# Left rows of Wo as partial sums per column tile, B rows and output in 128-token tiles, and one filler pass inside Wo, in a segment-recurrent attention kernel

## The chip, the cores and the metric

One core of one Trainium2 chip (trn2). The metric is the device time of one execution in microseconds (us). "Before" and "after" are the kernel without and with the change. Times are medians of several executions. Engines are named as in the profile: PE is TensorE's matmuls, PEld its weight loads, DVE is VectorE, ACT is ScalarE. To evict is to copy a finished product out of its accumulation bank. PV is the product of the attention weights with V; a segment has two, of 16 heads each.

## The reference, cut to what matters

Two attention branches over the same 2048 tokens of width 512 are mixed by a gate. Branch A is recurrent: 64 segments of 32 tokens, each with 8 memory tokens in front, 32 heads of 128. The first 8 output rows of a segment are the memory of the next.

```python
def _A_ref(x, mem0, Wq, Wk, Wv, Wo, seg_len):          # seg_len 32, M 8
    mem = mem0
    for s in range(n_seg):                             # 64, one after the other
        h = concat([mem, x[:, 32*s:32*s+32]], axis=1)  # 40 tokens
        q, k, v = h @ Wq, h @ Wk, h @ Wv               # 32 heads of 128
        p = softmax(where(mask, q k^T * scale, -1e9))
        o = einsum('bhte,hed->btd', p v, Wo)
        mem = o[:, :M]; outs.append(o[:, M:])
# b = _B_ref(...): 4 blocks of 512 tokens, ends in  o @ wo
g = sigmoid((x * gate_w).sum(-1))
return g * a + (1 - g) * b
```

## The kernel before

All of B but its last product is computed first, up to about 355 us. Then the segments run. A segment works on 32 tokens, the 8 memory rows and the first 24 of its own; the last 8 tokens of four segments, 32 rows, are done together as "left rows", in filler passes that stand in the next segments. Four segments make a group (r = 0 to 3 is the place in it). The filler units of a group are spread over 24 slots, six a segment.

A matmul on a token tile of 32 uses 32 columns of TensorE's array (128*32 in the profile's shapes; one on 128 tokens has 128*128), so the kernel works in four column tiles (j) side by side: in the trace before, a set of four matmuls of 512 columns on the four tiles started every 216 ns, and so did single ones of 128*128. For Wo each tile computes another 128 of the 512 output columns:

```python
def wo(b):                      # main Wo; b = 0, 1: heads 0-15, 16-31
    for half in range(2):
        for h in range(16*b + 8*half, 16*b + 8*half + 8):
            for j in range(4):
                pe.matmul(pb[bk][SEG*j:SEG*(j+1), 0:128], OT_sb[:, h, 0:SEG],
                          Wo_sb[:, h, 128*j:128*(j+1)], start=(h == 0), stop=(h == H-1))

def ol_units(g):                # left rows, four filler units of 8 heads
    ...
        for h in range(8*part, 8*part + 8):
            for j in range(4):
                pe.matmul(pb[bk][SEG*j:SEG*(j+1), 0:128], OTL[par][:, h, :],
                          Wo_sb[:, h, 128*j:128*(j+1)], ...)
        # after part 3: 16 matmuls for the left B rows, t1L (ACT), finL (DVE), four stores

# end of a segment
    scores(1); take_fill(2); sums(1)
    bks0 = pv(0)
    ot_ev(0, bks0, 1, "dve"); norm(1); ot_ev(0, bks0, 0, "act")
    brow(...)                   # 16 matmuls, B rows of these 32 tokens
    take_fill(2)
    # ACT: t1 = (1 - g) * B rows
    bks1 = pv(1)
    ot_ev(1, bks1, 0, "dve"); ot_ev(1, bks1, 1, "act")
    wo(0); wo(1)
    # DVE: aW = evicted Wo
    take_fill(1)
    # PE: transpose aW; DVE: its 8 memory columns into hT of the next segment
    take_fill(1)
    # DVE: fin = g * aW + t1; four stores every fourth segment
```

`take_fill(n)` issues the units of the next n slots. A matmul is two instructions, weight load and matmul (33,806 and 33,774 records in the profile before).

The softmax here doesn't subtract the row's maximum and nothing guards it: scores larger than these inputs give would overflow.

## Time and profile before

| | before |
|---|---|
| time, median (range) | 1375.42 us (1368.93 to 1380.39, 4 runs) |
| start of the first segment | 355 us |
| one group of four segments (trace, groups 2 to 15) | 63.6 us |
| TensorE instructions per group | about 3650 |
| instruction packets of 16 KB | 264 |

Lines of the profile's page: the span, busy time by engine with its share and the number of instructions, the DMA queues, and the chain that ended last.

```profile
span 1371.9 us, 72224 instructions
...
PE 1110.0 (81%) x33774; PEld 664.6 (48%) x33806; DVE 591.8 (43%) x1541; ACT 622.3 (45%) x1440; POOL 187.0 (14%) x416
...
q1 hardware_dynamic: 19496, 23.09, 4.9%
q8 instruction: 264, 4.33, 1.3%
...
PE 67%; DVE 11%; ACT 10%; issue 10%; DMA 2%; SPq 0%; POOL 0%; DVEq 0%; ACTq 0%
```

TensorE is the engine to look at. A tenth of the chain is "issue": time in which the engine waited for nothing that the profile knows. 264 packets on q8 for the 67,580 matmuls and weight loads are 256 instructions each.

The view of waits names who waited for whom: total us, number of times, longest.

```profile
PE ps L1088 <- issue: 69.5, 51, 2.1
...
DVE finL_sb L952 <- ACT t1L L949: 24.5, 16, 3.3
...
PE ps L873 <- DVE hT L1146: 15.8, 33, 0.8
...
PE ps L938 <- issue: 12.5, 10, 1.8
PE ps L1052 <- DVE Pn_sb L1040: 10.2, 34, 0.7
PE ps L873 <- issue: 7.3, 9, 1.5
```

L1088 is main Wo, L938 left Wo, L1052 the PV product, L873 the projections. The pauses before Wo come to 69.5 us in 51 pieces.

Matmuls of one segment (r = 0), in order of time: start, length, line, shapes, number; in brackets the idle time before.

```profile
865.15 0.41 PE L968 MATMUL ps<-woB_sb,oT 128*32 128x128 bf16 x16
...
865.94 0.89 PE L938 MATMUL ps<-Wo_sb,OTL 128*32 128x128 bf16 x49 [0.17 <-issue]
866.76 0.27 PE L1052 MATMUL ps<-Pn_sb,V_sb 32*128 32x40 bf16 x16
...
867.05 0.85 PE L1088 MATMUL ps<-Wo_sb,OT_sb 128*32 128x128 bf16 x47
869.27 1.35 PE L1088 MATMUL ps<-Wo_sb,OT_sb 128*32 128x128 bf16 x81 [1.37 <-issue]
...
872.74 0.23 PE L968 MATMUL ps<-woB_sb,oTL 128*32 128x128 bf16 x1 [1.50 <-issue]
```

The pauses cut through runs of identical matmuls whose inputs have long been there, so no data dependency explains them. Set beside the packet times on q8, the longer ones end 1.1 to 1.8 us after an instruction packet has landed: of the 85 weight-load gaps over 0.9 us in the recurrent part 69 do, and the other 16 end with a result of DVE or ACT. Counted in the built program, nearly all stand at the same place modulo 256 instructions: 68 of the 69 at remainder 194 or 195. A pause is therefore TensorE waiting for the next block of its own program. Packets start no closer than about 3.2 us apart and take 1.05 us in the mean, while a Wo of 256 instructions takes 1.8 us unstalled, a matmul every 14 ns. At each of the 68 pauses TensorE had used up all blocks landed, and in no trace did the packet of a block start while TensorE was more than 1.2 blocks short of it (at most 1.11 here).

From this I made one measure, used below as **stall**: at each block end of the recurrent part, the gap between weight loads, less 0.06 us, if it exceeds 0.15 us and ends 1.1 to 1.8 us after a landing. **Rest** is the segment's time less its stall. Both are means over the groups from the second on, by r, and are worked out from the trace; the profile prints neither.

| us | r=0 | r=1 | r=2 | r=3 | group |
|---|---|---|---|---|---|
| stall, before | 3.36 | 1.40 | 1.49 | 1.35 | 7.58 |
| rest, before | 14.30 | 13.94 | 13.56 | 13.84 | 55.63 |

### The profile page before, as it was taken

To read this page: it belongs to the slowest core of one execution; us is meant where nothing else is said; L and a number is where in the kernel's file an instruction comes from. 1 tells how busy PE (TensorE), PEld (TensorE's weight loads), DVE (VectorE), ACT (ScalarE), POOL (GpSimd) and SP (SyncE) were. 2 spreads that over 40 slices of the span, in tenths; PEclk is the share of its full clock that TensorE was granted. 3 is DMA by queue.
4 is the path that set the end of the run, shared out by engine and by line. 5 is a ranking of instruction groups with operands and counts; after the bars stand their busy time and mean duration, and the time that the engine had idled before them with its cause. 6 is when DMAs were issued, how large, how long until landed. Compare 5 with 4: busy or idle time off the path is not lost.

```text
span 1371.9 us, 72224 instructions
## 1 busy us (share of the span) xinstructions
PE 1110.0 (81%) x33774; PEld 664.6 (48%) x33806; DVE 591.8 (43%) x1541; ACT 622.3 (45%) x1440; POOL 187.0 (14%) x416
## 2 busy tenths in 40 slices
PE   4767667676788889888898988898888889798886
PEld 3444445344345555544555554454554455454544
DVE  3556667564343334433343433343433334343433
ACT  3857656474343434433344434343433444343433
POOL 7323222132001000010000000000010000000000
PEclk8988788576899999998999999999999999999999
DMA  9400000001100000000000000000000000000000
GB/s 358 135 2 3 2 2 2 2 2 52 75 4 8 5 6 7 5 7 4 7 5 8 3 9 4 7 7 4 7 5 7 4 8 4 7 4 8 3 7 8
DMA packets 19794, 27.70 MB, mean 20 GB/s; under 512 B 9760, under 2 KB 17960, under 8 KB 17960
## 3 DMA queue, kind: packets, MB, share of 16 engines
q1 hardware_dynamic: 19496, 23.09, 4.9%
q8 instruction: 264, 4.33, 1.3%
q14 instruction: 34, 0.28, 0.1%
HBM read 20.99 MB, written 2.10 MB: 17 GB/s over the span
## 4 chain that ended last, share of the span: by engine, by line
PE 67%; DVE 11%; ACT 10%; issue 10%; DMA 2%; SPq 0%; POOL 0%; DVEq 0%; ACTq 0%
PE ps L873 32%; PE ps L1088 10%; ACT PT_g L662 6%; PE ps L882 6%; PE ps L572 2%; PE ps L653 2%; PE ps L1052 2%; PE ps L938 2%; PE ps L1028 1%; PE ps L1008 1%; DVE OT_sb L865 1%; PE ps L968 1%; PE ps L1061 1%; DVE QTg L576 1%; DMA Wv_sb<-in_A_Wv_dram 1%
## 5 line engine op out<-in xcount | busy, mean ns | idle before, releaser
L662 ACT ACTIVATE PT_g<-ps 128x512 bf16<-128x512 f32 (+1 forms) x384 | 170.3, 529 | 58.1 <-PE ps L653 55.7
L1088 PE MATMUL ps<-Wo_sb,OT_sb 128*32 128x128 bf16 x8192 | 138.4, 220 | 69.6 <-issue 69.5
L1088 PEld LDWEIGHTS ps<-Wo_sb,OT_sb 128*32 128x32 bf16 x8192 | 117.9, 97 | 78.5 <-issue 76.7
L1133 POOL COPY OTL<-OT_sb 128x256 bf16<-128x256 bf16 x64 | 25.8, 403 | 920.1 <-DVE OT_sb L865 920.1
L873 PE MATMUL ps<-Wk_sb,hT 128*32 128x512 bf16 x2048 | 136.3, 406 | 17.7 <-DVE hT L1146 15.8
L873 PE MATMUL ps<-Wq_sb,hT 128*32 128x512 bf16 x2048 | 136.1, 382 | 0.0
L865 DVE CAST V_sb<-ps 128x512 bf16<-128x512 f32 x128 | 88.6, 692 | 110.0 <-PE ps L873 110.0
L873 PE MATMUL ps<-Wv_sb,hT 128*32 128x512 bf16 x2048 | 134.8, 381 | 0.0
L863 ACT ACTIVATE QN_sb<-ps 128x512 bf16<-128x512 f32 x128 | 76.5, 597 | 124.1 <-PE ps L873 124.1
L668 POOL TENSOR_SCALAR_AFFINE_SELECT PT_g<-PT_g 128x512 bf16<-128x512 bf16 x128 | 82.8, 647 | 211.8 <-ACT PT_g L662 209.6
L865 DVE CAST KN_sb<-ps 128x512 bf16<-128x512 f32 x64 | 44.3, 692 | 132.1 <-PE ps L873 132.1
L863 ACT ACTIVATE QT_sb<-ps 128x512 bf16<-128x512 bf16 x128 | 76.4, 597 | 45.4 <-PE ps L882 45.4
L873 PEld LDWEIGHTS ps<-Wk_sb,hT 128*32 128x32 bf16 x2048 | 55.2, 101 | 80.8 <-DVE hT L1146 26.8
L865 DVE COPY KT_sb<-ps 128x512 bf16<-128x512 bf16 x128 | 54.4, 425 | 88.4 <-PE ps L882 88.4
L865 DVE CAST aW_sb<-ps 128x128 bf16<-128x128 f32 x64 | 18.7, 292 | 171.1 <-PE ps L1088 171.1
L865 DVE CAST OT_sb<-ps 128x320 bf16<-128x320 f32 x128 | 63.0, 492 | 52.5 <-PE ps L1061 51.2
L653 PE MATMUL ps<-QTg,KTg 16*128 16x128 bf16 x1280 | 43.0, 244 | 52.1 <-ACT PT_g L662 48.6
L863 ACT ACTIVATE KN_sb<-ps 128x512 bf16<-128x512 f32 x64 | 38.2, 597 | 94.7 <-PE ps L873 94.7
L863 ACT ACTIVATE OT_sb<-ps 128x320 bf16<-128x320 f32 x128 | 55.0, 430 | 50.5 <-PE ps L1061 49.9
L873 PEld LDWEIGHTS ps<-Wq_sb,hT 128*32 128x32 bf16 x2048 | 50.8, 97 | 49.7 <-issue 3.4
L873 PEld LDWEIGHTS ps<-Wv_sb,hT 128*32 128x32 bf16 x2048 | 49.5, 95 | 30.4
L1031 ACT ACTIVATE R_sb<-ps 128x160 f32<-128x160 f32 x128 | 38.9, 304 | 54.4 <-PE ps L1029 54.3
(136 smaller groups left out, 1846.0 us busy)
## 6 DMA issues: line engine op xcount, KB each, us to landing
Wk_sb<-in_A_Wk_dram SPq DMA_DIRECT2D x4, 1024.0 KB, 11.6
Wq_sb<-in_A_Wq_dram SPq DMA_DIRECT2D x4, 1024.0 KB, 20.6
Wo_sb<-in_A_Wo_dram SPq DMA_DIRECT2D x4, 1024.0 KB, 19.7
Wv_sb<-in_A_Wv_dram SPq DMA_DIRECT2D x4, 1024.0 KB, 9.4
x_sb<-in_A_x_dram SPq DMA_DIRECT2D x4, 512.0 KB, 5.5
out_dram<-fin_sb SPq DMA_DIRECT2D x64, 24.0 KB
out_dram<-finL_sb SPq DMA_DIRECT2D x64, 8.0 KB
wqN_sb<-in_B_wq_dram SPq DMA_DIRECT2D x1, 512.0 KB, 7.3
```

The source lines that it names most:

```text
L572: ins = pe.matmul(pb[7][:, 0:LB], wqB_sb[:, c, g * 128:(g + 1) * 128], xT[:, c, T0p:T0p + LB], start=(c == 0), stop=(c == C - 1))
L653: ins = pe.matmul(pb[j][:, 128 * slot:128 * (slot + 1)], KTg[32 * j:32 * j + DH, 128 * kc:128 * kc + 128], QTg[32 * j:32 * j + DH, 128 * q ...
L662: P.op("act", (lambda j=j: (lambda a: a.activation(ptb[:, j, 128 * n0:128 * (n0 + len(wv))], pb[j][:, 0:128 * len(wv)], ACT.Exp, scale=SCA ...
L668: P.op("gp", (lambda n=n: (lambda gq: gq.affine_select(ptb[:, :, 128 * n:128 * (n + 1)], ptb[:, :, 128 * n:128 * (n + 1)], [[0, 4], [1, 128]],
L863: P.op("act", lambda a: a.activation(dst, src, ACT.Copy), reads=[rbank[k] for k in bks], writes=dres, name=name)
L865: P.op("dve", lambda d: d.tensor_copy(dst, src), reads=[rbank[k] for k in bks], writes=dres, name=name)
L873: ins = pe.matmul(pb[bk][SEG * j:SEG * (j + 1), :], lhs(c), w_sb[:, c, n0:n0 + 512], start=(c == 0), stop=(c == C - 1))
L882: ins = pe.transpose(pb16[bk][:, i * 128:(i + 1) * 128], nat[:, b, i * 128:(i + 1) * 128], ident[:, :])
L938: ins = pe.matmul(pb[bk][SEG * j:SEG * (j + 1), 0:128], OTL[par][:, h, :], Wo_sb[:, h, 128 * j:128 * (j + 1)], start=(h == 0), stop=(h == ...
L1031: P.op("act", lambda a: a.activation(R_sb[:, b, :], pb[bk][:, 224:384], ACT.Ln), reads=[rbank[bk]], writes=[Rs("R%d" % b)], name="ln%d_%d" ...
L1052: ins = pe.matmul(pb[bks[j]][:, L * i:L * (i + 1)], V_sb[SEG * j:SEG * (j + 1), b, i * E:(i + 1) * E], Pn_sb[SEG * j:SEG * (j + 1), b, L * ...
L1088: ins = pe.matmul(pb[bk][SEG * j:SEG * (j + 1), 0:128], OT_sb[:, h, 0:SEG], Wo_sb[:, h, 128 * j:128 * (j + 1)], start=(h == 0), stop=(h == ...
```

## The change

The intent: fewer and wider TensorE instructions for the same products, cheaper output, and something other than Wo matmuls in the middle of Wo. Left Wo: each column tile sums 8 of the 32 heads over all 512 columns, 32 matmuls of 512 columns instead of 128 of 128. The four partial sums (rows 32j to 32j+31) are evicted as a bf16 value and its rounding remainder, and a 0/1 matrix `selL` sums the four tiles and transposes at once. B rows: one unit of four matmuls per group on the 128 tokens. The output is collected transposed in `aT_st`, transposed back once per group, gated, and stored with one DMA. One of the two fillers between the PVs moves between `wo(0)` and `wo(1)`. The per-place gates, and the five fp32 matmuls that made them at the start, go. Its core, with cuts marked:

```diff
-                    for h in range(8 * part, 8 * part + 8):
+                    for n in (2 * part, 2 * part + 1):
                         for j in range(4):
-                            ins = pe.matmul(pb[bk][SEG * j:SEG * (j + 1), 0:128], OTL[par][:, h, :],
-                                            Wo_sb[:, h, 128 * j:128 * (j + 1)], start=(h == 0), stop=(h == H - 1))
+                            h = 16 * (n // 4) + 4 * j + n % 4
+                            ins = pe.matmul(pb[bk][SEG * j:SEG * (j + 1), :], OTL[par][:, h, :], Wo_sb[:, h, :],
+                                            start=(n == 0), stop=(n == 7))
...
                 if part == 3:
-                    ... (left B rows, t1L, finL, four stores)
+                    evac("act", LN_sb[:, 0, :], pb[bk], [bk], [rl[0]], "olhi%d" % g)
+                    P.op("dve", lambda d: d.tensor_tensor(LN_sb[:, 1, :], pb[bk], LN_sb[:, 0, :], ALU.subtract), ...)
...
+        def ut():   # 8 matmuls: LN_sb[:, k, 128c:128c+128] with selL -> ACT copies the left columns into aT_st
+        def ub():   # 4 matmuls of 512 columns: B rows; ACT: t1 = (1 - g) * B rows, 128x512
+        def uf():   # 4 transposes of aT_st; DVE: fin = g * aT + t1, 128x512; one store
...
         ot_ev(0, bks0, 0, "act")
-        bb = B.take()
-        brow(bb, lambda f: oT[:, f, SEG * s:SEG * (s + 1)], ...)
-        take_fill(2)
-        P.op("act", ... t1 ...)
+        take_fill(1)
         bks1 = pv(1)
...
         wo(0)
+        take_fill(1)
         wo(1)
...
+        P.op("dve", lambda d: d.tensor_copy(aT_st[par][:, :, SEG * r:SEG * (r + 1) - M], asrc[:, :, M:SEG]), ...)
         take_fill(1)
-        fb = fin_sb
-        P.op("dve", ... fin ...)
-        if r == 3 or s == nseg - 1:
-            ... (four stores)
```

## The prediction

> What bounds it. The change touches the recurrent part, from about 355 us to the end: 64 segments, 15.8 us each. TensorE is the bottleneck: from 500 to 1360 us it was busy 748 of 860 us (windows view), DVE 335, ACT 357. A segment is about 13.8 us of TensorE work and dependency gaps, and up to 2 us of "issue": in the waits view TensorE idled 70 us before the Wo matmuls, 12 before the left-row Wo, 17 before others, 98 us in all, with nothing to wait for. The DMA view names the cause: queue q8, kind instruction, moved 264 packets of 16 KB for 67,600 TensorE instructions, 256 each. A long pause ends about 1.3 us after such a packet, nearly always at the same place of the 256. Wo is 128 matmuls and 128 weight loads in 1.8 us: it eats a block faster than the next arrives. [...]

> What changes, per group of four segments.
> Instructions: left Wo 128 to 32 pairs, B rows 80 to 4, plus 8 for the selecting transpose and 4 for the output transpose: 160 pairs fewer, about 3650 to 3333 instructions, 14.3 to 13.0 blocks. The filler inside Wo (none in one segment of four) lets a block arrive meanwhile.
> Charging each block what a fetch of about 3.5 us exceeds the time of its 256 instructions, I get about 8 us of stall per group before and 3.5 after: gain 4.5 us.
> TensorE work stays nearly equal: left Wo 32 x 57 ns is still 1.8 us, B rows 4 x 216 ns replace 5 x 0.23 us; about 0.5 us of selection and 0.2 us of transposes are new.
> Dependencies get worse. Between first and second PV stands a DVE chain of 1.44 us whatever fills it. Before, the B rows and one or two fillers hid there; now one, and what left (three fillers a group in Wo, 0.5 us each) stands on the path: +1.5 us. In a group's first segment the high/low split (ACT 0.6 us, DVE 0.7 us) precedes the copy of the new memory and the selection: +0.8 us. In the second, the 128x512 t1 (0.6 us) and fin (0.7 us) delay the evictions between the PVs: +1 us. Loss about 3.4 us.
> Net -1.1 us per group, -18 us over 16. At the start five gate selection matmuls (2.3 us) and a copy go: -2.6 us. Tail: zero.

> Predicted 1357 us (-1.6%), 8 in 10 within 1332 to 1380. Faster by over 2%: 0.36; within 2%: 0.60; slower: 0.04.

> Would show it right: instruction packets near 245; issue time before Wo down by more than half; left Wo pauses nearly gone; longer waits of the second PV on DVE and of the next K on hT; about 15.4 us per segment.

> Would make it wrong: if the fetch stall nearly vanishes, the gain is 4%. If it only moves to PV or projection instructions, or the DVE and ACT queues delay the PVs more than I add up, there is no gain. Stalls depend on where blocks end; 3333 is nearly 13 blocks, so these places hardly drift, and a bad one repeats.

The sum: -4.5 us of stall and +3.4 us of loss make -1.1 us per group, -18 us over 16 groups, with -2.6 us at the start. The 3.5 us of a fetch is an estimate; in the recurrent part of the trace before, packets start 3.2 us apart at the least, and one in ten within 3.5 us.

## The result, and the profile after

After: 1338.44 us (1335.08 to 1341.21, 4 runs); before 1375.42 us. The ratio is 0.9733, 95% interval 0.9681 to 0.9785.

The page after:

```profile
span 1339.3 us, 67341 instructions
...
PE 1098.6 (82%) x31189; PEld 645.9 (48%) x31237; DVE 600.9 (45%) x1556; ACT 621.8 (46%) x1408; POOL 173.7 (13%) x399
...
q1 hardware_dynamic: 12584, 23.09, 4.7%
q8 instruction: 244, 4.00, 1.2%
...
PE 68%; DVE 13%; ACT 10%; issue 7%; DMA 2%; SPq 0%; DVEq 0%; POOL 0%; ACTq 0%
```

20 instruction packets fewer; TensorE's busy time hardly moved (1110 to 1099 us) while the span fell by 33. The work is nearly the same, and the pauses went. "Issue" fell to 7% of the chain and DVE rose to 13%.

The waits after (L1099 main Wo, L923 left Wo, L1063 PV, L941 the selection matmuls):

```profile
PE ps L1063 <- DVE Pn_sb L1051: 44.9, 60, 1.4
PE ps L1099 <- issue: 29.5, 28, 1.8
PE ps L941 <- DVE hT L1154: 17.5, 14, 1.3
PE ps L854 <- DVE hT L1154: 5.0, 19, 0.3
PE ps L923 <- issue: 1.2, 3, 0.7
```

Pauses before Wo fell from 69.5 to 29.5 us, before left Wo from 12.5 to 1.2. In return the second PV waits 44.9 us on DVE (10.2 before), and the selection matmuls 17.5 us. The end of a segment with r = 0 shows the latter, all engines:

```profile
796.00 0.60 PE L923 MATMUL ps<-Wo_sb,OTL 128*32 128x512 bf16 x8
796.30 0.29 DVE L846 CAST aW_sb<-ps 128x128 bf16<-128x128 f32 x1 [1.75 <-PE ps L1099]
...
796.65 0.23 PE L1150 MATMUL ps<-ident,aW_sb 128*128 128x128 bf16 x1
796.66 0.60 ACT L844 ACTIVATE LN_sb<-ps 128x512 bf16<-128x512 f32 x1 [2.24 <-PE ps L923]
797.29 0.69 DVE L929 TENSOR_TENSOR LN_sb<-ps,LN_sb 128x512 bf16<-128x512 f32 x1 [0.70 <-ACT LN_sb L844]
797.90 0.17 DVE L1154 COPY hT<-ps 128x32 bf16<-128x32 bf16 x1
...
798.13 0.35 PE L941 MATMUL ps<-selL,LN_sb 128*128 128x32 bf16 x8 [1.25 <-DVE hT L1154]
798.41 1.91 PE L854 MATMUL ps<-Wk_sb,hT 128*32 128x512 bf16 x32
```

The transpose of the new memory was issued at 796.65, but its copy into hT (L1154) started only at 797.90: on DVE the remainder (L929) stood in front of it, and that waited for ACT. The next segment's K waits behind all of it.

The same kernel was run again as a control beside the first experiments (1340.79 us, ratio 0.9723). Its table against before:

| us | r=0 | r=1 | r=2 | r=3 | group |
|---|---|---|---|---|---|
| stall, control | 0.44 | 0.34 | 1.50 | 1.40 | 3.67 |
| rest, control | 15.03 | 14.48 | 14.08 | 14.10 | 57.69 |
| change of stall | -2.92 | -1.06 | +0.01 | +0.05 | -3.91 |
| change of rest | +0.73 | +0.54 | +0.52 | +0.27 | +2.06 |

So the change takes 3.9 us of stall from a group and adds 2.1 us of rest: 1.85 us net, 30 of the 33 us between the profiles. The profiled run after gave a stall of 2.90 and a total of 61.3 us, so the stall of one kernel varies from execution to execution.

The rest holds one thing more, shown under e1: stretches in which TensorE's granted clock was 0.5 in the records instead of 1.0. Between the first segment and the end the clock records hold 8 such intervals before (31 us together), 1 in the control (3.4 us) and 7 in the profiled run after (24 us). If half of such time is lost (an estimate, for work that fills it), the rest is 54.7 us per group before and 57.6 in both others: the change adds 2.9 us of dependencies, more than the table says. Over the whole recurrent part it takes away 75 us of stall in the profiled run after and 63 in the control, and 3 or 14 us of lost clock; so the stall is the gain in both.

### The profile page after: what moved, and what is told of

It is laid out like the page before. It is cut to its first block, busy times and chain, and to the rows that moved or that the text cites. A ratio compares the mean times of both kernels' runs of the same rounds, so it can differ in the third digit from the quotient of the medians.

```text
span 1339.3 us, 67341 instructions
## 1 busy us (share of the span) xinstructions
PE 1098.6 (82%) x31189; PEld 645.9 (48%) x31237; DVE 600.9 (45%) x1556; ACT 621.8 (46%) x1408; POOL 173.7 (13%) x399
## 4 chain that ended last, share of the span: by engine, by line
PE 68%; DVE 13%; ACT 10%; issue 7%; DMA 2%; SPq 0%; DVEq 0%; POOL 0%; ACTq 0%
PE ps L854 33%; PE ps L1099 10%; ACT PT_g L643 6%; PE ps L863 6%; PE ps L553 2%; PE ps L1063 2%; PE ps L634 2%; PE ps L1019 2%; DVE Pn_sb L1049 1%; PE ps L1039 1%; PE ps L1072 1%; PE ps L923 1%; DVE QTg L557 1%; PE ps L958 1%; DVE V_sb L846 1%
## 5 line engine op out<-in xcount | busy, mean ns | idle before, releaser
L1099 PE MATMUL ps<-Wo_sb,OT_sb 128*32 128x128 bf16 x8192 | 142.7, 221 | 29.5 <-issue 29.5
L1099 PEld LDWEIGHTS ps<-Wo_sb,OT_sb 128*32 128x32 bf16 x8192 | 123.1, 97 | 45.0 <-issue 35.2
L854 PE MATMUL ps<-Wk_sb,hT 128*32 128x512 bf16 x2048 | 131.3, 400 | 6.3 <-DVE hT L1154 5.0
L1063 PE MATMUL ps<-Pn_sb,V_sb 32*128 32x40 bf16 x2048 | 35.6, 177 | 47.3 <-DVE Pn_sb L1051 44.9
```

The costliest lines, as they stand in the source:

```text
L854: ins = pe.matmul(pb[bk][SEG * j:SEG * (j + 1), :], lhs(c), w_sb[:, c, n0:n0 + 512], start=(c == 0), stop=(c == C - 1))
L1063: ins = pe.matmul(pb[bks[j]][:, L * i:L * (i + 1)], V_sb[SEG * j:SEG * (j + 1), b, i * E:(i + 1) * E], Pn_sb[SEG * j:SEG * (j + 1), b, L * ...
L1099: ins = pe.matmul(pb[bk][SEG * j:SEG * (j + 1), 0:128], OT_sb[:, h, 0:SEG], Wo_sb[:, h, 128 * j:128 * (j + 1)], start=(h == 0), stop=(h == ...
```

## The experiments

Theory: TensorE waits for blocks of its program; the gain is the smaller instruction demand, and the loss is that of dependencies on DVE and ACT. Rivals: the gain comes from the work taken off DVE, ACT and the stores; or from the filler in Wo; or the pauses belong to places in the segment. Every kernel here computed the correct result.

| kernel | median us | ratio to before (95%) | stall / rest per group, profiled run |
|---|---|---|---|
| e0_control (after) | 1340.79 | 0.9723 (0.9683 to 0.9763) | 3.67 / 57.69 |
| e1_narrow_left | 1395.48 | 1.0129 (1.0083 to 1.0174) | 5.38 / 59.31 |
| e2_filler_back | 1329.59 | 0.9647 (0.9608 to 0.9686) | 3.42 / 57.15 |
| e4_queue_order | 1297.82 | 0.9430 (0.9387 to 0.9473) | 3.48 / 55.03 |
| b1_filler_in_wo | 1369.77 | 0.9989 (0.9959 to 1.0020) | 6.75 / 56.18 |
| e7_narrow_brows | 1363.77 | 0.9946 (0.9909 to 0.9982) | 4.26 / 58.24 |
| e3b_shift64 | 1358.94 | 0.9862 (0.9817 to 0.9908) | 3.51 / 57.88 |
| e3_shift128 | 1363.53 | 0.9929 (0.9887 to 0.9972) | 3.72 / 58.84 |
| e3c_shift192 | 1348.09 | 0.9804 (0.9760 to 0.9848) | 3.81 / 58.01 |
| e4s_shift128 | 1332.62 | 0.9650 (0.9603 to 0.9698) | 4.93 / 55.60 |
| e5b_wide_main | 1262.51 | 0.9207 (0.9173 to 0.9241) | 0.08 / 56.05 |
| e5c_wide_shift128 | 1265.21 | 0.9183 (0.9142 to 0.9223) | 0.15 / 56.06 |

Compare ratios across groups of runs, not medians: the kernel before itself had medians of 1371.79 to 1378.71 in them.

### e0_control: the change again

> The changed kernel again, for comparison on the same chip as the next three. Every theory: about 0.973 of the kernel before, 1338 us.

0.9723, as expected. Two of its waits, to which e2 is compared:

```profile
PE ps L1063 <- DVE Pn_sb L1051: 44.8, 60, 1.4
...
PE ps L1099 <- issue: 37.9, 30, 1.8
```

### e1_narrow_left: only the instruction count of left Wo undone

```diff
-                            ins = pe.matmul(pb[bk][SEG * j:SEG * (j + 1), :], OTL[par][:, h, :], Wo_sb[:, h, :],
-                                            start=(n == 0), stop=(n == 7))
+                            for w in range(4):
+                                ins = pe.matmul(pb[bk][SEG * j:SEG * (j + 1), 128 * w:128 * (w + 1)], OTL[par][:, h, :],
+                                                Wo_sb[:, h, 128 * w:128 * (w + 1)], start=(n == 0 and w == 0), ...)
```

> The changed kernel with each 512-wide matmul of the left Wo rows cut into four of 128 columns: same columns streamed, same sums, same everything else, only 96 matmuls and 96 weight loads more per group of four segments. Theory (TensorE waits for instruction blocks of 256; a block costs about 3.5 us): block count goes from 13.0 to 13.8 per group, issue time before Wo and left Wo rises by about 2 us per group, 1370 us (+31), ratio to before about 0.996; 12 instruction packets more. Rival (the gain came from what left DVE, ACT and the stores, and TensorE pays by columns): within 5 us of the control.

Direction confirmed, size not: 1395.48 us, 55 above the control where 31 was expected, and slower than the kernel before. Stall rose by 1.7 us per group as expected (about 2), the packets to 257 (by 13), and the rival is out: the columns streamed, DVE, ACT and the stores were untouched. But the rest rose by 1.6 us too, which the theory did not have. The timeline shows where:

```profile
621.58 0.85 PE L1101 MATMUL ps<-Wo_sb,OT_sb 128*32 128x128 bf16 x48 [0.64 <-issue]
622.25 0.66 PE L924 MATMUL ps<-Wo_sb,OTL 128*32 128x128 bf16 x32
622.90 0.23 PE L1152 MATMUL ps<-ident,aW_sb 128*128 128x128 bf16 x1
624.46 0.37 PE L943 MATMUL ps<-selL,LN_sb 128*128 128x32 bf16 x8 [1.33 <-DVE hT L1156]
624.76 3.45 PE L854 MATMUL ps<-Wk_sb,hT 128*32 128x512 bf16 x32
```

The two K passes take 3.45 us; after 798.41 in the trace shown above the same 32 matmuls took 1.91. The busy times by stretch, with the granted clock third from the end of a row:

```profile
624.00:628.00 4.00, 3.54 (x40) 1.54 (x44) 0.51 (x3) 0.88 (x2) 0.00 (x0) 0.57 0.02 4
628.00:634.00 6.00, 6.00 (x152) 2.97 (x144) 2.58 (x5) 2.84 (x6) 0.00 (x0) 1.00 0.00 0
```

The clock was down here, 0.57 in the first row against 1.00 in the second. The trace's clock records of the recurrent part hold 17 half-clock intervals, 68 us together, against one of 3.4 us in the control (and 8, 31 us, in the kernel before). At most half of the extra 65 us is lost (an estimate, for work that fills the interval), about 30 us, which fits the missing 1.6 us per group: less that half, the rest is 57.2 us against 57.6 in the control, so the added instructions cost stall and clock and nothing else that shows. These intervals are 3.41 us or twice that. TensorE was not idle ahead of them: in the 3.41 us just before, it was busy for 21 to 66% of the time (28 to 48% in the kernel before, 41 to 61% in the profiled run after).

### e2_filler_back: the filler out of Wo

```diff
-        take_fill(1)
+        take_fill(2)
         bks1 = pv(1)
...
         wo(0)
-        take_fill(1)
         wo(1)
```

> The changed kernel with the filler pass taken out of the middle of Wo and put back between first and second PV (two there, as before). Theory: there it fills idle time for nothing, in Wo it stands on the path; TensorE idle at the second PV falls by about 1.2 us per group, issue time rises by about 0.8, so 7 us faster than the control (0 to 14). Rival (the filler in Wo is what removes the stalls): slower than the control by over 15 us.

11 us faster than the control (median; ratios 0.9647 and 0.9723). The second PV's wait on DVE shrank from 44.8 us in the control to 19.0:

```profile
PE ps L1099 <- issue: 38.9, 35, 2.1
PE ps L1063 <- DVE Pn_sb L1051: 19.0, 20, 1.1
```

The issue time did not rise (37.9 in the control), where I had expected some. The rival falls: the filler in Wo is a cost here. Stall did not rise without it (3.67 to 3.42 us per group), and the rest fell by 0.5, or by 1.0 less half the half-clock time (about 20 us in this trace). Between the PVs the filler used time that was idle anyway.

### b1_filler_in_wo: that part of the change alone

The same move in the other direction, made in the kernel before (`take_fill(2)` to `take_fill(1)` between the PVs, `take_fill(1)` between `wo(0)` and `wo(1)`).

> The kernel before with one part of the change alone: one of the two filler passes moves from between the PVs into the middle of Wo. Theory: it gives a block time to arrive (stall 0.7 us less per group) and stands on the path (0.8 us more): within 10 us of the kernel before. Rival (this is the part that gains): faster by 20 us or more.

Ratio 0.9989: nothing. Stall fell by 0.83 us per group and rest rose by 0.55, close to the two terms expected.

### e4_queue_order: the same instructions in another order

Built on e2. The eviction of left Wo becomes a unit of its own, and the full groups use a fixed order of slots:

```diff
+        if len(q) == 22:
+            ol0, ol1, ol2, ol3, ue, ut, ub, uf, K00, K01, K10, K11, Q00, TK, Q01, Q10, Q11, V00, TQ, V01, V10, V11 = q
+            slots = [ol0, None, ol1, ol2, ol3, ue,
+                     ut, K00, K01, None, K10, ub,
+                     uf, K11, Q00, TK, Q10, Q01,
+                     Q11, V00, TQ, V10, V11, V01]
```

(`ue` is the split on ACT and DVE, now issued after the memory copy.)

> e2 with the filler units in another order, so that nothing long stands on DVE or ACT ahead of what the path waits for: the high/low split after the copy of the new memory and its selection one segment part later, t1 and fin no longer ahead of the PV evictions, no left K eviction on DVE ahead of the memory copy. Same instructions. Theory (about 2 us per group are lost to those queues in the first two segments): 20 to 35 us faster than e2, about 1305 us; wait of the next K on hT and of the second PV in segment two back to the values of the other segments. Rival (those queues were off the path, the loss is TensorE work): within 5 us of e2.

1297.82 us, 32 below e2. The rest fell from 57.15 to 55.03 us per group, 2.1 us as expected (1.9 less half the half-clock time) and back to that of the kernel before. The place shown above for r = 0 now reads:

```profile
777.13 0.23 PE L1152 MATMUL ps<-ident,aW_sb 128*128 128x128 bf16 x1
777.15 0.60 ACT L844 ACTIVATE LN_sb<-ps 128x512 bf16<-128x512 f32 x1 [2.17 <-PE ps L923]
777.40 0.17 DVE L1156 COPY hT<-ps 128x32 bf16<-128x32 bf16 x1 [0.32 <-PE ps L1152]
777.49 0.20 DVE L1158 COPY aT_st<-ps 128x96 bf16<-128x96 bf16 x1
777.63 0.77 PEld L854 LDWEIGHTS ps<-Wk_sb,hT 128*32 128x32 bf16 x20 [0.40 <-DVE hT L1156]
777.63 1.05 PE L854 MATMUL ps<-Wk_sb,hT 128*32 128x512 bf16 x16 [0.27 <-DVE hT L1156]
777.78 0.69 DVE L932 TENSOR_TENSOR LN_sb<-ps,LN_sb 128x512 bf16<-128x512 f32 x1
```

From the transpose to the next K are 0.50 us instead of 1.76 (at r = 0 the mean was 0.96 before the change, 1.68 after it, 0.50 here). The subtraction is as long as before and nobody waits for it. The rival (TensorE work) falls.

### e7_narrow_brows: only the instruction count of the B rows undone

```diff
-                    ins = pe.matmul(pb[bb], oT[:, f, 128 * g:128 * (g + 1)], woB_sb[:, f, :], start=(f == 0), ...)
+                    for w in range(4):
+                        for r in range(4):
+                            ins = pe.matmul(pb[bb][SEG * r:SEG * (r + 1), 128 * w:128 * (w + 1)],
+                                            oT[:, f, 128 * g + SEG * r:128 * g + SEG * (r + 1)], woB_sb[:, f, 128 * w:128 * (w + 1)], ...)
```

> The changed kernel with the B rows of a group again as 64 matmuls of 32 tokens by 128 columns instead of 4 of 128 by 512; same place, same columns per tile. Theory (instruction count): 120 instructions more per group, stall 0.5 us more per group, 8 us slower than the changed kernel (0 to 20). Rival (wide B rows are the main gain): over 25 us slower.

A miss in size: 0.9946, against 0.9723 for the control, which is some 30 us where 8 was expected, and more than the rival's 25 us too. In the profiled run, the fastest of its six and 17 us above the control's, stall rose by 0.59 us per group, 9 us in 16 groups and near the expected 8, and half-clock intervals took 27 us against 3. So the stall term was right, and a second cost came on top, as in e1: half of the added half-clock time is 12 us (an estimate), and the two together are already more than the 17. For the slower executions there is no trace.

### e3_shift128: where the blocks end

64 small matmuls once, ahead of the first segment:

```diff
+        for _ in range(64):
+            ins = pe.matmul(pb[pbk][:, 0:32], ident[:, :], ident[:, 0:32], start=True, stop=True)
```

> The changed kernel with 64 small matmuls, 128 instructions, once ahead of the recurrent part; nothing in the loop changes. Theory: stalls sit where blocks of 256 end, so they move. Charging 3.55 us per block gave stalls of 0.6, 0.3, 1.6, 1.0 us in the four segments of a group for the changed kernel (its control showed 0.4, 0.3, 1.5, 1.4); shifted it gives 1.6, 0.8, 0.7, 0.7. Total time within 12 us of the changed kernel. Rival (the pauses belong to a place in the segment, such as a buffer or queue that runs full): stalls stay in the third and fourth segment.

The mechanism held. Stalls by r went from 0.44, 0.34, 1.50, 1.40 to 1.60, 1.20, 0.21, 0.71 us, with the same sum (3.67 and 3.72). A pause tied to a place in the segment would have stayed. The time did not hold: 0.9929, about 25 us slower than the changed kernel where at most 12 was expected. The clock records hold 12 half-clock intervals (48 us, against 3.4 in the control). Half of the difference is 22 us, and the first segment began 4.5 us later: together 3 us more than the 24 between the two profiled runs.

### e4s_shift128: the shift where the first segment has no idle time

The same insertion ahead of e4.

> The same 128 instructions once ahead of the recurrent part, now ahead of e4, where nothing long delays the memory copy in the first segment of a group. The shift cost the changed kernel about 20 us although its stalls kept their sum; its records show 12 half-clock intervals there against 1 in the control. Theory (stalls that fall next to the idle time of the first segment let the clock drop, and the half clock is what cost the time; e4 has no such idle time): stalls move to the first two segments, by the same charging 0 to 1 us more per group, half-clock intervals stay under 7, and the time is 0 to 16 us above e4, ratio to the kernel before 0.943 to 0.955. Rival (the shift costs by itself, for instance by stalls on the recurrent path): again 20 us or more above e4, with few half-clock intervals.

My theory fell in part. The shift cost e4 35 us (ratio 0.9650 against 0.9430). Stalls moved to 2.27, 1.57, 0.47, 0.61 us by r, and their sum rose from 3.48 to 4.93, more than I allowed, which is 23 us over 16 groups. Half-clock intervals were 10 (34 us), not under 7, against 3 (10 us) in e4, without the idle time that I had held to be needed. Half of the added half-clock time is 12 us, and 23 + 12 is the whole difference between the two profiled runs, 35 us. The rival is right about the size and wrong about the clock. What is shown: the place of the block ends alone, with the same loop, is worth 35 us here by the medians, 30 by the ratios.

### e3b_shift64 and e3c_shift192: more offsets

32 and 96 small matmuls in place of 64.

> The changed kernel shifted by 64 instructions (32 small matmuls ahead of the recurrent part). My theory on e4s fell in part: the shift raised the stall there by 1.4 us per group and half-clock intervals came back. Now: the loop of 3333 instructions nearly repeats its block ends, so each offset is a fixed draw. By the charging of 3.55 us per block stalls are 0.6, 1.7, 1.0, 0.7 us in the four segments, 4.0 per group (3.5 unshifted): 5 to 30 us above the changed kernel, ratio to the kernel before 0.977 to 0.995. Rival (offset does not matter, 128 was an accident of the added matmuls): 0.968 to 0.976.

> The changed kernel shifted by 192 instructions (96 small matmuls). Same charging: 1.0, 0.2, 0.5, 1.6 us, 3.3 per group, none of it in segment two: within 10 us of the changed kernel, ratio 0.966 to 0.982, although more matmuls were added than in the 128 case. Rival (the added matmuls cost): worse than the 128 case, above 0.993.

0.9862 and 0.9804, both inside the ranges. Of the three insertions the largest costs the least, clear of the noise against that of 64 matmuls (0.9929), so it is the offset that counts and not the added matmuls. The profiled run of e3b was the fastest of its five (1349.72 us at a mean clock of 0.941; the slowest 1363.21 at 0.927), so its low stall of 3.51 is not typical of the median. The changed kernel at four offsets is at 0.972, 0.986, 0.993 and 0.980 of before, 0.983 in the mean.

### e5b_wide_main: the idea carried to the main Wo

Built on e4. Each column tile sums 8 heads over two banks of 256 columns:

```diff
-                    for h in range(16 * b + 8 * half, 16 * b + 8 * half + 8):
-                        for j in range(4):
-                            ins = pe.matmul(pb[bk][SEG * j:SEG * (j + 1), 0:128], OT_sb[:, h, 0:SEG],
-                                            Wo_sb[:, h, 128 * j:128 * (j + 1)], start=(h == 0), stop=(h == H - 1))
+                    for n in range(2):
+                        for w in range(2):
+                            for j in range(4):
+                                h = 16 * b + 8 * half + 2 * j + n
+                                ins = pe.matmul(pb[bk[w]][SEG * j:SEG * (j + 1), 0:256], OT_sb[:, h, 0:SEG],
+                                                Wo_sb[:, h, 256 * w:256 * (w + 1)], ...)
...
-        evac("dve", aw[:, :], pb[wb["bk"]][:, 0:128], [wb["bk"]], [raw], "aW%d" % s)
+        evac("dve", aw[:, 0:256], pb[wb["bk"][0]][:, 0:256], [wb["bk"][0]], [raw], "aW%d" % s)
+        evac("act", aw[:, 256:512], pb[wb["bk"][1]][:, 0:256], [wb["bk"][1]], [raw2], "aWb%d" % s)
...
-        P.op("pe", lambda pe: pe.transpose(pb16[bk][:, 0:128], aw[:, :], ident[:, :]), ...)
+            for c in range(C):
+                ins = pe.matmul(pb[bk][:, SEG * c:SEG * (c + 1)], aw[:, 128 * c:128 * (c + 1)], selL[:, :], start=True, stop=True, ...)
```

The partial sums are rounded to bf16 once here, without the remainder; the result was still correct.

> Built on e4: the change's idea carried to the main Wo. Each column tile sums 8 of the 32 heads over two banks of 256 columns, 64 matmuls instead of 128; DVE and ACT each evict one bank, and four matmuls with the selection matrix sum and transpose at once, in place of one transpose. 512 instructions fewer per group, 2.8k. Theory: stall from 3.5 to about 0.5 us per group, path longer by 0.3 to 0.5 us per segment; 15 to 35 us faster than e4, about 1273 us. Rival (by now the stalls are hidden behind something else): no faster than e4.

1262.51 us, ratio 0.9207, 35 us below e4 by the medians and 31 by the ratios: the fastest kernel that was tried, shifted (e5c, below) or not. Lines of its page:

```profile
span 1260.8 us, 59696 instructions
...
PE 1095.5 (87%) x27333; PEld 631.0 (50%) x27333; DVE 613.7 (49%) x1556; ACT 645.4 (51%) x1472; POOL 173.8 (14%) x399
...
q8 instruction: 214, 3.51, 1.1%
```

TensorE's busy time is what it was (1099 after the change, 1095 here) and its share of the span has risen to 87%. Stall is 0.08 us per group, and the recurrent part has no half-clock interval. The longer path costs 1.0 us of rest per group against e4.

### e5c_wide_shift128: the shift without stalls

The 64 small matmuls ahead of e5b.

> e5b shifted by 128 instructions. Theory (without stalls there is nothing to shift): within 5 us of e5b, ratio 0.917 to 0.926, stall under 0.3 us per group, no half-clock intervals. Rival (shift costs of itself): 20 us above e5b.

0.9183, as fast as e5b: with no stall there is nothing to shift. Together with e4s this rules out that the shift costs by itself.

## Why the prediction was right or wrong

The time, 1338 us, lay inside the range of 1332 to 1380, 19 us below the stated 1357; that it was faster by over 2% had been given 0.36. The direction, the cause and the two opposing terms were right, one of them too large by about 0.5 us, and a third term, the clock, was missing.

- "Gain 4.5 us" of stall per group: 3.9 us in the control, 4.7 in the profiled run after (7.58 less 2.90). Right. Packets (244), left Wo pauses (12.5 to 1.2 us) and the mean segment of the profiled run (15.3 us, "about 15.4") came as said. The issue time before Wo fell by 58% in that run but by 45% in the control, so "more than half" holds for one of two.
- "Loss about 3.4 us": the rest rose by 2.06 us in the control and by 2.8 in the profiled run after, and by 2.9 in both once half of the half-clock time is taken off (an estimate). The queues were sized right: charged 0.8 and 1.0 us, and e4 took back 1.9 by order alone. At r = 0 the time from the transpose to the next K rose by 0.72 us, where 0.8 was charged for the split. The fillers in Wo were mis-sized: charged 1.5 us, and taking them out (e2) gave back 1.0. Both takings together are the 2.9, so the loss was these two and not TensorE work.
- "Net -1.1 us per group": -1.85 in the control, which is 3.9 of stall and 0.8 of clock less 2.9; about -1.9 in the profiled run after, 4.7 and 0.1 less 2.9. Two executions of one kernel differed in stall and in clock and hardly in their sum.
- "At the start ... -2.6 us": the first score matmuls of B did start 2.6 us earlier (32.74 to 30.18 us), but the first segment only 0.6 us earlier (354.67 to 354.04). The starts of the recurrent part lay between 352 and 356 us in runs without a shift, so 2 us can't be told there.
- "These places hardly drift, and a bad one repeats": shown by the shifts. It also says how the 2.7% is to be read. The kernel before, with about 3652 instructions per group, takes other block ends in every group; the changed one nearly keeps its own (3333 is 5 over 13 blocks, a drift of about 75 instructions over the run), and at the other three offsets tried it is 0.7 to 2.0% faster than before. That the mean of the four, 1.7%, lies by the stated 1.6% is no proof of the sum.
- Not foreseen at all: the half clock. e1, e7, e3 and e4s cost more than their stalls, each with 7 to 17 half-clock intervals; the kernel before had 8. Stall over the recurrent part, half of the half-clock time and the start of the first segment, added up (an estimate), give differences of 60, 20, 26 and 34 us to the control (for e4s to e4), where 56, 17, 24 and 35 were measured between the profiled runs. The last group, which took 64 to 72 us there against 59 in the control and in e4, is of the same kind: in e3, for instance, 5.5 us of stall and 5.1 of lost clock make its 10.6 more.

## What to carry to other kernels

A dense run of narrow matmuls can be bound by the delivery of its own instructions (here 7.6 us of 63 in a group before): look for "issue" pauses inside runs of equal instructions, and count instructions per microsecond of work against the packets of the instruction queue. Widen the moving operand, letting column tiles hold partial sums and one small matmul add them, rather than put other work inside the dense run (e5b took 35 us off e4; the filler in Wo cost 11). Before a term is sized from two traces, take the half-clock time out of both: here it hid over a quarter of the loss. And when a long operation joins a filler, look at what stands behind it in the DVE and ACT queues: the same instructions in another order were worth 32 us here, nearly as much as the change itself (37).
